# Layer 2's weights prepared during layer 1's blocks and kept in DRAM, and VectorE or GpSimd chosen operation by operation in the first block

## The chip, the core and the metric

The kernel runs on one core of a Trainium2 chip. The metric is the device time of one execution in microseconds (us). The profile is of one execution on that core. Engine names in rows: PE is TensorE, PEld its weight load, DVE is VectorE, ACT is ScalarE, POOL is GpSimd, SP is SyncE, which issues every DMA here.

## What is computed

A linear attention on 8 batches of 576 tokens (8 heads of 64), then two gated layers on the 4608 tokens, each 512 wide:

```
q_s = exp(q - max_d q);  q_s /= sum_d q_s
k_s = exp(k - max_s k);  k_s /= sum_s k_s
x   = q_s @ (k_s^T @ v)                      # per batch and head -> 4608 x 512
x   = (sigmoid(x @ w_gate) * (x @ w_val)) @ w_out      # 512 -> 1536 -> 512
h   = x @ w_in                                          # 512 -> 2048
out = ((a0 + a1 h + a2 h^2 + a3 h^3) / (1 + |b0||h| + |b1| h^2 + 1e-6)) @ w_out2
```

The layers' weights arrive as 64-bit numbers; the kernel makes 32-bit values of them with bit operations.

## The kernel before

**Products.** Each operand of a product is split into a high part (rounded by a copy on ScalarE) and a low part (value minus high part), and a product is three matmuls: high by high, low by high, high by low (`mm3`). One matmul covers 128x128 weights and 512 columns.

**Blocks and steps.** The 4608 tokens are 9 blocks of 512. In layer 1 a block has 12 steps, one for each 128 of the 1536 hidden units (`f`). Step `i` stands in this order on TensorE: the 24 matmuls of `front_a` (gate `pg` and value `pv`), what the attention of the next block puts there, and the 12 matmuls of `back_a` of the step before. Behind `front_a` come the sigmoid on ScalarE (L398), the multiplication by `pv` on VectorE (`sg`, L400, called the gate below), and the split of the result into `gh` (ScalarE) and `gl`. `pg` and `pv` have two PSUM buffers in all, so the next step's `front_a` waits for this sigmoid and this gate.

**Attention.** Blocks 1 to 7 of layer 1 also carry the attention of the block behind, in four units of two heads at fixed steps of a block (`UNIT_STEPS`). In an even step stand the exponentials of a unit (ScalarE, with a table load ahead and one behind), the normalisation of its queries on VectorE, and the maxima and subtraction of the next unit (`km`, `qm`, `q`). In the odd step behind it TensorE transposes the key maxima (`ps_kt`), multiplies keys by values (`ps_kv`), transposes the queries (`ps_qt`), runs `back_a`, and transposes the maxima back (`ps_kb`). These four share two PSUM buffers: `ps_qt` waits until VectorE has read `ps_kt` (`mx`, L281), `ps_kb` until VectorE has read `ps_kv` (`kvl`, L349).

**Weight pieces.** A piece of weights is 128 x 512. Layer 1 has 36 pieces, layer 2 has 32. Preparing one takes a load of 512 KB, an absolute value on ScalarE (L188), two TENSOR_SCALAR (L194, L197) and two SCALAR_TENSOR_TENSOR (L204, L207) on VectorE, the copy to the high part `wh` on ScalarE and the subtraction to the low part `wl` on GpSimd. Layer 1's pieces are prepared in block 0. Layer 2's are prepared in layer 1's last block (block 8), because their 64 tiles take the places of layer 1's weights in SBUF as these are used up:

```
want = 0
if j == NBLK - 2:
    want = NW1
elif j == NBLK - 1:
    want = NW1 + 3 * f + (2 if f == 0 else 1)
run(prep(min(want, NW), 3), sequence(vec, work.get(i, [])))
```

**Block 0.** Its operations (attention of blocks 0 and 1, the weights, the 12 steps) are a list with dependences; `in_time` walks through it with a cost for each kind of operation and emits the order in which every engine's queue gets its work. The engine of each kind is fixed: `wl`, `gl`, the key subtraction and the query division go to GpSimd, with the exceptions in `Q_SUB_ON_DVE` and one key subtraction.

Of the kernel before, what the change touches and what calls it, by code (L numbers as in the profile page):

```python
# [35 lines left out]
Q_SUB_ON_DVE = ((0, 0), (0, 1), (1, 0), (1, 1), (1, 2), (1, 3))  # L36
# [4 lines left out]
    "load_k": (DMA, 0.92), "load_q": (DMA, 0.74), "load_v": (DMA, 0.92), "load_w": (DMA, 1.46), "load_ab": (DMA, 0.06),  # L41
    "k_max": (DVE, 1.25), "k_t": (PE, 0.2), "k_mx": (DVE, 0.3), "k_mb": (DVE, 0.2), "k_b": (PE, 0.2),
    "k_cp": (ACT, 0.33), "k_sub": (POOL, 1.5), "k_exp": (ACT, 0.63, "exp"),
    "q_max": (DVE, 0.6), "q_sub": (POOL, 1.0), "q_exp": (ACT, 0.63, "exp"),
    "q_sum": (DVE, 0.6), "q_add": (DVE, 0.07), "q_inv": (DVE, 0.12), "q_div": (POOL, 1.0),
    "kv": (PE, 1.1), "kv_add": (DVE, 0.07), "kv_inv": (DVE, 0.12), "kv_h": (ACT, 0.4), "kv_l": (DVE, 0.4),
    "qt": (PE, 0.43), "qt_h": (ACT, 0.52), "qt_l": (DVE, 0.6),
    "x": (PE, 0.65), "x_h": (ACT, 0.52), "x_l": (DVE, 0.6),
    "xa": (PE, 0.65), "xa_out": (ACT, 0.2), "xb": (PE, 0.65), "xb_out": (ACT, 0.5),
    "w_abs": (ACT, 0.52), "w_clip": (DVE, 0.34), "w_cut": (DVE, 0.34), "w_low": (DVE, 0.6), "w_sign": (DVE, 0.6),  # L50
    "w_h": (ACT, 0.52), "w_l": (POOL, 1.23),
    "front": (PE, 1.3), "sig": (ACT, 0.48, "sigmoid"), "gate": (DVE, 0.6), "g_h": (ACT, 0.52), "g_l": (POOL, 1.23),
# [7 lines left out]
def in_time(ops, on_dve):  # L60
# [8 lines left out]
    def kind(o):  # L69
        eng, cost, table = (*KINDS[o[0]], None)[:3]  # L70
        return (DVE, DVE_COST[o[0]], table) if o in on_dve else (eng, cost, table)

    def lag(a, b):
        return 0.0 if kind(a)[0] == kind(b)[0] != DVE else LATENCY[kind(a)[0]]

    def length(o):
        if o not in rest:
            rest[o] = kind(o)[1] + max([lag(o, x) + length(x) for x in followers[o]], default=0.0)
        return rest[o]

    ready = {o: 0.0 for o, (_, after) in ops.items() if not after}
    free = dict.fromkeys(LATENCY, 0.0)
    table = "exp"
    while ready:
        starts = []
        for eng in free:
# [19 lines left out]
def kernel(ctx: ExitStack, tc: tile.TileContext, q, k, v, w1, w2, ab_in, out):  # L106
# [20 lines left out]
    ab = const.tile([P, 6], F32, name="ab")  # L127
# [14 lines left out]
    x_raw = xpool.tile([P, KC, NB], F32, name="x_raw")  # L142
    x3_d = [dram.tile([KC, P, NB], F32, name=f"x3_{j}") for j in range(NBLK)]
# [31 lines left out]
    late_pool = []  # L175
    done = [NW1] * 5
# [5 lines left out]
    def prep_abs(p):  # L182
        if p < NW1 - 2:
            val[p] = early[(p + 2) % 6]
        else:
            pool = stage if p < NW1 else late_pool[0]
            val[p] = pool.tile([P, NB], F32, tag="val", name="val", bufs=1 if p < NW1 else 4)
        nc.scalar.activation(val[p], raw[p][:, :, 1].bitcast(F32), AF.Abs)  # L188
# [22 lines left out]
    def prep_split(p):  # L211
        wt[p] = [wpool.tile([P, NB], F32R, tag="w", name=n) for n in ("wh", "wl")]
        yield from split_steps(*wt[p], val.pop(p), nc.gpsimd)

    def prep(until, times=1):

        for _ in range(times):
            jobs = []
            for n in (4, 3, 2, 1, 0):
                ready = done[n - 1] if n else len(pieces)  # L220
                if n == 0 and done[0] - done[3] >= STAGES:
                    continue
# [52 lines left out]
    def att_kt(j, u, pool, tag):  # L275
# [4 lines left out]
        mx = att.tile([P, 1], F32, tag="mx", name="mx")  # L280
# [13 lines left out]
    def att_qm(j, u):  # L294
        qm[j, u] = att.tile([P, 8], F32, tag="qm", name="qm", bufs=3)
# [100 lines left out]
    def vec_a(j, f, pg, pv):  # L396
# [8 lines left out]
        yield from split_steps(gh, gl, sg, nc.gpsimd if j in (0, NBLK - 1) and f < NF1 - 1 else nc.vector)  # L405
# [41 lines left out]
    def pool_or_dve(name):  # L447
        return nc.vector if name in on_dve else nc.gpsimd

    on_dve = {("k_sub", 0, 0)} | {("q_sub", *x) for x in Q_SUB_ON_DVE}  # L450
    banks = [("kv", 0, 0), ("qt", 0, 0)]
    for i in range(2 * NHP):
# [41 lines left out]
    for p in range(NW1):  # L494
# [5 lines left out]
        chain([("w_h", p), ("w_l", p)], prep_split(p), ("w_sign", p), p and ("w_h", p - 1))  # L500
# [27 lines left out]
    for kk in range(KC):  # L528
        chain([("next_h", kk), ("next_l", kk)], split_steps(x_h[:, kk, :], x_l[:, kk, :], x_raw[:, kk, :], nc.vector),
              ("front", NF1 - 1, KC - 1), ("xb_out", 1, kk))  # L530
# [3 lines left out]
    for o in in_time(ops, on_dve):  # L534
# [37 lines left out]

    NA = NBLK * NF1
    pend = [(0, NF1 - 1)]
    for i in range(NF1, NA):
# [14 lines left out]
        want = 0  # L590
        if j == NBLK - 2:
            want = NW1
        elif j == NBLK - 1:
            want = NW1 + 3 * f + (2 if f == 0 else 1)
        run(prep(min(want, NW), 3), sequence(vec, work.get(i, [])))
# [6 lines left out]
        if i == NA - NF1 - 2:  # L602
            att_ctx.close()
            late_pool.append(stage_ctx.enter_context(tc.tile_pool(name="late", bufs=4)))


    while done[4] < NW:
        run(prep(NW))
# [82 lines left out]
    for i in range(NBS + LAG):  # L691
        if i < NBS:
# [58 lines left out]
```

## Time and profile before

| | us |
|---|---|
| median of 3 runs | 1855.32 (1854.53 to 1855.99) |
| the profiled execution, its own time | 1856.38 |
| span of its profile | 1854.6 |
| time outside the span in that execution | 1.78 |
| TensorE busy in the span | 1783.7 |
| VectorE busy | 1224.2 |
| ScalarE busy | 1007.9 |
| GpSimd busy | 392.1 |
| granted TensorE clock, mean | 0.992 |

Engines work side by side, so busy times do not add up to the span. A matmul's duration overlaps with the next one's; the pace of TensorE is read from the starts of two matmuls and the number between them. Block 0 ends at about 185 us, block 8 of layer 1 begins at 942.17 us, and layer 2 has its first output matmul at 1077.79 us.

### The profile page before, as it was taken

The page shows a single profiled execution, that of the slowest core. Times are in us where ns is not written, and L with a number is a line of the kernel's source. Part 1 is how long each engine was busy: PE and PEld are TensorE (multiplying, and loading weights), DVE is VectorE, ACT ScalarE, POOL GpSimd, SP SyncE. Part 2 cuts the span into 40 slices and gives each one's busy share as a digit, 9 for nine tenths or more (in the row PEclk, how much of TensorE's full clock was granted, in tenths as well). Part 3 has the DMA queues.
Part 4 walks back from the last instruction along what each step waited for, and adds up shares of the span by engine and source line. Part 5 has one row for each costly group of instructions (what it writes and reads, how often), then busy time and mean ns, then how long its engine had stood idle before and what let it go on. Part 6 is the DMA issues. An engine that isn't in the chain of part 4 may idle for free.

```text
span 1854.6 us, 22112 instructions
## 1 busy us (share of the span) xinstructions
PE 1783.7 (96%) x8384; PEld 1458.1 (79%) x8384; DVE 1224.2 (66%) x1907; ACT 1007.9 (54%) x1656; POOL 392.1 (21%) x297
## 2 busy tenths in 40 slices
PE   5879999999999999999998899999999999999999
PEld 3657888888888888888876688888888888888887
DVE  9997443434344353433369988888888888787876
ACT  4546343433434343333334487777776767676765
POOL 4664000101000000100025522222222222222222
PEclk9989999999999999999999999999999999999999
DMA  5452111101011110211024210000100000000000
GB/s 203 149 166 63 63 41 44 60 23 60 21 63 41 43 60 8 77 47 46 6 96 166 102 46 24 24 24 23 46 10 37 23 23 23 23 24 23 1 23 24
DMA packets 39563, 95.97 MB, mean 52 GB/s; under 512 B 4128, under 2 KB 4128, under 8 KB 39456
## 3 DMA queue, kind: packets, MB, share of 16 engines
q1 hardware_dynamic: 39456, 94.55, 15.2%
q8 instruction: 66, 1.08, 0.2%
q14 instruction: 41, 0.34, 0.1%
HBM read 75.66 MB, written 18.87 MB: 51 GB/s over the span
## 4 chain that ended last, share of the span: by engine, by line
PE 83%; DVE 12%; issue 3%; ACT 2%; DMA 1%; POOL 0%; DVEq 0%; ACTq 0%; SPq 0%
PE accb L672 21%; PE acc L414 13%; PE ph L155 7%; PE ph L157 7%; PE ph L156 7%; PE pv L155 4%; PE pv L157 4%; PE pg L155 4%; PE pv L156 4%; PE pg L156 4%; PE pg L157 4%; DVE sg L400 1%; DVE early L207 1%; DVE val L194 1%; DVE early L204 1%
## 5 line engine op out<-in xcount | busy, mean ns | idle before, releaser
L148 POOL TENSOR_TENSOR glb<-gb,ghb 128x512 fp32r<-128x512 f32 x144 | 186.8, 1297 | 594.3 <-ACT ghb L146 594.3
L400 DVE TENSOR_TENSOR sg<-pv,sg 128x512 f32<-128x512 f32 x108 | 74.4, 689 | 332.2 <-PE pv L157 171.3
L398 ACT ACTIVATE sg<-pg 128x512 f32<-128x512 f32 x108 | 64.4, 596 | 363.1 <-PE pg L157 359.4
L640 ACT ACTIVATE h<-ph 128x512 f32<-128x512 f32 x144 | 86.1, 598 | 197.1 <-PE ph L157 195.9
L155 PE MATMUL pv<-x_h,wh 128*128 128x512 f32 x432 | 172.3, 399 | 17.6 <-DVE sg L400 17.5
L155 PE MATMUL pg<-x_h,wh 128*128 128x512 f32 x432 | 175.1, 405 | 13.5 <-ACT sg L398 13.3
L308 POOL TENSOR_TENSOR k<-k,kma 128x640 f32<-128x640 f32 x29 | 46.4, 1600 | 599.2 <-ACT kma L291 599.2
L157 PE MATMUL pg<-x_l,wh 128*128 128x512 f32 x432 | 170.6, 395 | 0.9 <-DVE x_l L381 0.9
L157 PE MATMUL pv<-x_l,wh 128*128 128x512 f32 x432 | 171.0, 396 | 0.0
L156 PE MATMUL pv<-x_h,wl 128*128 128x512 f32 x432 | 170.9, 396 | 0.0
L156 PE MATMUL pg<-x_h,wl 128*128 128x512 f32 x432 | 170.8, 395 | 0.0
L672 PE MATMUL accb<-wl,ghb 128*128 128x512 f32 x576 | 158.3, 389 | 0.0
L672 PE MATMUL accb<-wh,ghb 128*128 128x512 f32 x576 | 158.3, 389 | 0.0
L672 PE MATMUL accb<-wh,glb 128*128 128x512 f32 x576 | 158.3, 389 | 0.0
L643 DVE SCALAR_TENSOR_TENSOR ah<-h,babs,ah 128x512 f32<-128x512 f32 x144 | 107.9, 749 | 53.8 <-ACT ah L641 53.8
L414 PE MATMUL acc<-gh,wh 128*128 128x512 f32 x432 | 125.5, 400 | 3.6 <-DVE x_raw L420 2.0
L155 PE MATMUL ph<-x_h,wh 128*128 128x512 f32 x320 | 124.6, 389 | 2.0 <-ACT x_h L146 2.0
L672 PEld LDWEIGHTS accb<-wh,glb 128*128 128x128 f32 x576 | 108.2, 188 | 22.4
L672 PEld LDWEIGHTS accb<-wl,ghb 128*128 128x128 f32 x576 | 108.1, 188 | 22.5
L672 PEld LDWEIGHTS accb<-wh,ghb 128*128 128x128 f32 x576 | 108.1, 188 | 22.4
L659 DVE SCALAR_TENSOR_TENSOR u<-ah,r 128x512 f32<-128x512 f32 x144 | 99.4, 690 | 39.5 <-ACT r L649 39.5
L157 PE MATMUL ph<-x_l,wh 128*128 128x512 f32 x320 | 124.6, 390 | 0.0
(118 smaller groups left out, 4045.3 us busy)
## 6 DMA issues: line engine op xcount, KB each, us to landing
raw<-in_w SPq DMA_DIRECT2D x68, 512.0 KB, 3.7
v<-in_v SPq DMA_DIRECT2D x30, 325.0 KB, 3.0
k<-in_k SPq DMA_DIRECT2D x30, 320.0 KB, 3.5
q<-in_q SPq DMA_DIRECT2D x36, 256.0 KB, 3.6
x<-x_raw SPq DMA_DIRECT2D x36, 256.0 KB, 2.2
x_raw<-x SPq DMA_DIRECT2D x9, 1024.0 KB, 5.5
out<-ob SPq DMA_DIRECT2D x36, 256.0 KB, 2.4
x_raw<-in_v SPq DMA_DIRECT2D x2, 325.0 KB, 4.9
```

What stands on the lines that cost most here:

```text
L148: lo_eng.tensor_tensor(out=lo, in0=src, in1=f32(h), op=ALU.subtract)
L155: nc.tensor.matmul(ps, wh, xh, start=first, stop=False)
L156: nc.tensor.matmul(ps, wl, xh, start=False, stop=False)
L157: nc.tensor.matmul(ps, wh, xl, start=False, stop=last)
L308: eng.tensor_tensor(out=t, in0=t, in1=kmt[j, u].unsqueeze(1).to_broadcast([P, KCH, P]), op=ALU.subtract)
L398: nc.scalar.activation(sg, pg, AF.Sigmoid)
L400: nc.vector.tensor_tensor(out=sg, in0=pv, in1=sg, op=ALU.mult)
L414: nc.tensor.matmul(accs["a", j][m], x[:, m * P:(m + 1) * P], y, start=(f == 0 and n == 0), stop=(f == NF1 - 1 and n == 2))
L640: nc.scalar.activation(h2, ph, AF.Square)
L643: nc.vector.scalar_tensor_tensor(out=ah, in0=h2, scalar=babs[:, 1:2], in1=ah, op0=ALU.mult, op1=ALU.add)
L659: nc.vector.scalar_tensor_tensor(out=u, in0=ah, scalar=q_one, in1=r, op0=ALU.add, op1=ALU.mult)
L672: nc.tensor.matmul(accs["b", j][t], x[:, t * P:(t + 1) * P], y, start=(f == 0 and n == 0), stop=(f == NF2 - 1 and n == 2))
```

## The change

**Layer 2's weights.** The 32 pieces are prepared during blocks 1 to 7, from step 14 of layer 1 on, one piece every two and a half steps: the load in its first step, the absolute value and the two TENSOR_SCALAR in the second, the two SCALAR_TENSOR_TENSOR, the high copy and the low subtraction (GpSimd) in the third. High and low part go into one staging tile `hl`, which a DMA writes to DRAM (`w2_d`). In block 8, when the tiles of layer 1's weights come free, `fetch` reads them back with two DMAs a piece; the last three pieces are fetched at layer 2's first step. The pool `late` and the preparation in block 8 go away.

**Block 0.** The costs in `KINDS` are other numbers, and six kinds (`k_sub`, `q_sub`, `q_div`, `w_l`, `g_l`, `next_l`) have a cost for VectorE and one for GpSimd. `in_time` takes the engine on which an operation would end first and notes it in `chosen`; `Chosen` emits it there. Four tiles are made larger (`ab`, `v`, `mx`, and one more buffer for `qm`).

```
-Q_SUB_ON_DVE = ((0, 0), (0, 1), (1, 0), (1, 1), (1, 2), (1, 3))
...
+    "w_h": (ACT, 0.62), "w_l": ({DVE: 0.7, POOL: 1.29},),
+    "g_l": ({DVE: 0.7, POOL: 1.29},),
...
+        for t, eng, mine in sorted(starts, key=lambda x: x[0]):
+            mine = [
+                o for o in mine
+                if all(t + engines(o)[eng] <= max(free[e], at(o, e)) + c for e, c in engines(o).items())]
+            if mine:
+                break
...
+    w2_d = [dram.tile([P, 2, NB], F32, name=f"w2_{p}") for p in range(2 * NF2)]
...
+    def prep_split(p, eng=nc.gpsimd):
+        if p < NW1:
+            wt[p] = [wpool.tile([P, NB], F32R, tag="w", name=n) for n in ("wh", "wl")]
+            yield from split_steps(*wt[p], val.pop(p), eng)
+        else:
+            hl = stage.tile([P, 2, NB], F32R, tag="raw", name="hl")
+            yield from split_steps(hl[:, 0], hl[:, 1], val.pop(p), nc.gpsimd)
+            yield
+            nc.sync.dma_start(out=w2_d[p - NW1], in_=f32(hl))
+
+    def fetch(p):
+        wt[p] = [wpool.tile([P, NB], F32R, tag="w", name=n) for n in ("wh", "wl")]
+        for n in range(2):
+            nc.sync.dma_start(out=f32(wt[p][n]), in_=w2_d[p - NW1][:, n])
+
+    def prep(stage_of):
+        for p, n in stage_of:
+            yield from (prep_load, prep_abs, prep_bits_a, prep_bits_b, prep_split)[n](p) or ()
+            yield
...
+    prep_at = {}
+    for p in range(NW1, NW):
+        at0 = NF1 + 2 + 5 * (p - NW1) // 2
+        for n, step in enumerate((0, 1, 1, 2, 2)):
+            prep_at.setdefault(at0 + step, []).append((p, n))
...
-        run(prep(min(want, NW), 3), sequence(vec, work.get(i, [])))
+        run(prep(prep_at.get(i, [])), sequence(vec, work.get(i, [])))
...
+        if j == NBLK - 1:
+            while len(wt) < NW and order1[len(wt) - NW1][0] < f - 1:
+                fetch(len(wt))
```

**Where it moves instructions.** In block 0 GpSimd has 64 operations before: 36 `wl`, 11 `gl`, 8 query divisions, 2 query subtractions and 7 key subtractions. With the change it has 46: 23, 10, 2, 5 and 6. The other 18 stand on VectorE.

The first place is ScalarE's queue in step 28 (block 2, an even step). Before (L398 is first the sigmoid, then the table load for the next one; `x_raw` is the attention's output, `k` and `q` the exponentials):

```order
L398 ACTIVATE sg<-pg 128x512
L146 ACTIVATE gh<-sg 128x512
L383 ACTIVATE x_raw<-ps_xt 128x192
L383 ACTIVATE x_raw<-ps_xt 128x320
L312 ACT_TABLE_LOAD
L312 ACTIVATE k<-k 128x640
L304 ACTIVATE q<-q 128x512
L398 ACT_TABLE_LOAD
```

With the change (ScalarE, the same step):

```order
L413 ACTIVATE sg<-pg 128x512
L160 ACTIVATE gh<-sg 128x512
L398 ACTIVATE x_raw<-ps_xt 128x192
L160 ACTIVATE hl<-val 128x512
L398 ACTIVATE x_raw<-ps_xt 128x320
L327 ACT_TABLE_LOAD
L327 ACTIVATE k<-k 128x640
L319 ACTIVATE q<-q 128x512
L413 ACT_TABLE_LOAD
```

The high copy of a weight piece (`hl`) now stands ahead of the table load and the exponentials, and it needs both SCALAR_TENSOR_TENSOR of its piece.

The second place is VectorE's queue in step 31 (block 2, an odd step). Before:

```order
L400 TENSOR_TENSOR sg<-pv,sg 128x512
L281 TENSOR_REDUCE mx<-ps_kt 128x1
L283 COPY km<-mx 128x128
L148 TENSOR_TENSOR gl<-sg,gh 128x512
L338 TENSOR_SCALAR rs<-ps_kv 128x1
L340 RECIPROCAL rs<-rs 128x1
L349 SCALAR_TENSOR_TENSOR kvl_105<-ps_kv,rs,kvh_97 64x64 x2
L364 TENSOR_TENSOR ql<-ps_qt,qh 128x512
```

With the change (VectorE, the same step):

```order
L415 TENSOR_TENSOR sg<-pv,sg 128x512
L296 TENSOR_REDUCE mx<-ps_kt 128x1
L298 COPY km<-mx 128x128
L215 SCALAR_TENSOR_TENSOR val<-raw,val 128x512
L218 SCALAR_TENSOR_TENSOR val<-raw,val 128x512
L162 TENSOR_TENSOR gl<-sg,gh 128x512
L353 TENSOR_SCALAR rs<-ps_kv 128x1
L355 RECIPROCAL rs<-rs 128x1
L364 SCALAR_TENSOR_TENSOR kvl_105<-ps_kv,rs,kvh_97 64x64 x2
L379 TENSOR_TENSOR ql<-ps_qt,qh 128x512
```

Two operations on a weight piece now stand ahead of `gl`, `rs` and `kvl`.

The third place is VectorE's queue at the end of block 0. Before, ahead of the block's last gate (the last row):

```order
L319 TENSOR_SCALAR qs<-qs 128x8
L321 RECIPROCAL qs<-qs 128x8
L338 TENSOR_SCALAR rs<-ps_kv 128x1
L400 TENSOR_TENSOR sg<-pv,sg 128x512
L340 RECIPROCAL rs<-rs 128x1
L349 SCALAR_TENSOR_TENSOR kvl_105<-ps_kv,rs,kvh_97 64x64 x2
L364 TENSOR_TENSOR ql<-ps_qt,qh 128x512
L338 TENSOR_SCALAR rs<-ps_kv 128x1
L340 RECIPROCAL rs<-rs 128x1
L364 TENSOR_TENSOR ql<-ps_qt,qh 128x512
L349 SCALAR_TENSOR_TENSOR kvl_106<-ps_kv,rs,kvh_98 64x64 x2
L400 TENSOR_TENSOR sg<-pv,sg 128x512
```

With the change (VectorE, the rows ahead of the same gate):

```order
L472 TENSOR_TENSOR wl<-val,wh 128x512
L205 TENSOR_SCALAR val<-val 128x512
L208 TENSOR_SCALAR val<-val 128x512
L353 TENSOR_SCALAR rs<-ps_kv 128x1
L215 SCALAR_TENSOR_TENSOR val<-raw,val 128x512
L355 RECIPROCAL rs<-rs 128x1
L218 SCALAR_TENSOR_TENSOR val<-raw,val 128x512
L379 TENSOR_TENSOR ql<-ps_qt,qh 128x512
L364 SCALAR_TENSOR_TENSOR kvl_106<-ps_kv,rs,kvh_98 64x64 x2
L472 TENSOR_TENSOR x_l<-x_raw,x_h 128x512 x3
L415 TENSOR_TENSOR sg<-pv,sg 128x512
```

Before, the last weight operation stands 13 rows ahead of the last gate (just ahead of these rows), with another gate between; now it stands four rows ahead of the last gate, with no gate between.

## Rows read from the trace of the kernel before

**Rows 1.** The page, part 1 (busy us, share, instructions) and VectorE's line of part 2.
```profile
PE 1783.7 (96%) x8384; PEld 1458.1 (79%) x8384; DVE 1224.2 (66%) x1907; ACT 1007.9 (54%) x1656; POOL 392.1 (21%) x297
DVE  9997443434344353433369988888888888787876
```

**Rows 2.** Stretches; columns: length, each engine's busy us, PEclk, DMA share, GB/s.
```profile
185.00:942.17 757.17, 751.17 (x3821) 619.64 (x3820) 303.58 (x577) 283.65 (x475) 37.70 (x24) 1.00 0.13 43
920.00:940.00 20.00, 20.00 (x92) 16.52 (x91) 3.65 (x6) 4.46 (x9) 0.00 (x0) 1.00 0.00 0
1000.00:1020.00 20.00, 16.66 (x70) 12.49 (x68) 19.86 (x24) 8.63 (x15) 11.31 (x8) 1.00 0.55 192
```

**Rows 3.** Timeline of TensorE, layer 1's last block and the first output step of layer 2.
```profile
934.01 0.39 PE L155 MATMUL pg<-x_h,wh 128*128 128x512 f32 x1
...
942.17 0.39 PE L155 MATMUL pg<-x_h,wh 128*128 128x512 f32 x1
...
1077.79 1.07 PE L672 MATMUL accb<-wh,ghb 128*128 128x512 f32 x4
```

**Rows 4.** What TensorE waited for, 940 to 1080 us; us in total, times, longest.
```profile
PE pv L155 <- DVE sg L400: 7.7, 6, 1.9
```

**Rows 5.** VectorE by line and shape, 0 to 166 us; busy us, mean ns, idle before.
```profile
L207 DVE SCALAR_TENSOR_TENSOR early<-raw,early 128x512 uint32<-128x512 uint32 x34 | 34.3, 1015 | 0.0
L204 DVE SCALAR_TENSOR_TENSOR early<-raw,early 128x512 uint32<-128x512 uint32 x34 | 27.2, 804 | 0.0
L194 DVE TENSOR_SCALAR early<-early 128x512 f32<-128x512 f32 x34 | 24.2, 718 | 0.0
L197 DVE TENSOR_SCALAR early<-early 128x512 uint32<-128x512 uint32 x34 | 23.8, 704 | 0.1
```

**Rows 6.** L194 on VectorE over the whole span; duration ns as minimum, median, maximum.
```profile
L194 DVE TENSOR_SCALAR early<-early x34: 366/416/1670, 22.8 to 145.3; 128x512 f32<-128x512 f32 x34
L194 DVE TENSOR_SCALAR val<-val x34: 414/1502/1535, 152.0 to 1057.6; 128x512 f32<-128x512 f32 x34
```

**Rows 7.** Timeline of VectorE at the end of block 0.
```profile
166.55 0.68 DVE L207 SCALAR_TENSOR_TENSOR val<-raw,val 128x512 uint32<-128x512 uint32 x1
...
183.12 0.69 DVE L400 TENSOR_TENSOR sg<-pv,sg 128x512 f32<-128x512 f32 x1 [1.24 <-ACT sg L398]
183.78 1.29 DVE L148 TENSOR_TENSOR x_l<-x_raw,x_h 128x512 fp32r<-128x512 f32 x2
```

**Rows 8.** The stretch between those operations, columns as in Rows 2.
```profile
167.23:183.12 15.89, 15.89 (x110) 12.95 (x109) 4.55 (x16) 10.74 (x20) 5.09 (x4) 1.00 0.20 60
```

**Rows 9.** What TensorE waited for, 0 to 170 us.
```profile
PE pg L155 <- ACT sg L398: 10.1, 5, 3.2
PE pv L155 <- DVE sg L400: 9.8, 5, 2.8
```

**Rows 10.** Timeline of ScalarE in a step with exponentials, block 1.
```profile
226.95 0.64 ACT L383 ACTIVATE x_raw<-ps_xt 128x128 f32<-128x128 f32 x2
227.61 1.28 ACT L312 ACT_TABLE_LOAD   x1
```

**Rows 11.** Timeline of VectorE in that step and the one behind it.
```profile
225.69 0.69 DVE L400 TENSOR_TENSOR sg<-pv,sg 128x512 f32<-128x512 f32 x1 [5.71 <-ACT sg L398]
...
230.20 0.69 DVE L317 TENSOR_REDUCE qs<-q 128x8 f32<-128x512 f32 x1 [2.42 <-ACT q L304]
...
234.78 0.69 DVE L400 TENSOR_TENSOR sg<-pv,sg 128x512 f32<-128x512 f32 x1 [0.18 <-PE ps_kt L278]
...
236.16 0.69 DVE L148 TENSOR_TENSOR gl<-sg,gh 128x512 fp32r<-128x512 f32 x1 [0.24 <-ACT gh L146]
...
237.88 0.58 DVE L349 SCALAR_TENSOR_TENSOR kvl<-ps_kv,rs,kvh 64x64 fp32r<-64x64 f32 x2 [0.76 <-ACT kvh L345]
```

**Rows 12.** Timeline of TensorE in the step behind it.
```profile
235.81 0.63 PE L357 MATMUL ps_qt<-ident,q 128*128 128x128 f32 x4 [0.30 <-DVE mx L281]
...
239.05 0.27 PE L288 MATMUL ps_kb<-ident,km 128*128 128x128 f32 x1
```

More of the change, by code (lines that the diff above doesn't have):

```diff
@@ L67, in in_time, with engines, table_of, at @@
     rest, end = {}, {}
[L69 to L74, printed above, removed]
+    def engines(o):
+        kind = KINDS[o[0]]
+        return kind[0] if isinstance(kind[0], dict) else {kind[0]: kind[1]}
+    def table_of(o):
+        return (*KINDS[o[0]], None, None)[2] if isinstance(KINDS[o[0]][0], str) else None
     def length(o):
         if o not in rest:
-            rest[o] = kind(o)[1] + max([lag(o, x) + length(x) for x in followers[o]], default=0.0)
+            rest[o] = min(engines(o).values()) + max([0.2 + length(x) for x in followers[o]], default=0.0)
         return rest[o]
-    ready = {o: 0.0 for o, (_, after) in ops.items() if not after}
+    ready = {o: (0.0, None) for o, (_, after) in ops.items() if not after}
     free = dict.fromkeys(LATENCY, 0.0)
     table = "exp"
+    def at(o, eng):
+        t, by = ready[o]
+        return t if by != eng or eng == DVE else t - LATENCY[eng]
     while ready:
@@ L126 @@
     make_identity(nc, ident)
-    ab = const.tile([P, 6], F32, name="ab")
+    ab = const.tile([P, 70], F32, name="ab")[:, :6]
     babs = const.tile([P, 2], F32, name="babs")
@@ L185, in prep_abs @@
         else:
-            pool = stage if p < NW1 else late_pool[0]
-            val[p] = pool.tile([P, NB], F32, tag="val", name="val", bufs=1 if p < NW1 else 4)
+            val[p] = stage.tile([P, NB], F32, tag="val", name="val", bufs=1)
         nc.scalar.activation(val[p], raw[p][:, :, 1].bitcast(F32), AF.Abs)
@@ L404, in vec_a @@
         g_t["a", j, f] = (gh, gl)
-        yield from split_steps(gh, gl, sg, nc.gpsimd if j in (0, NBLK - 1) and f < NF1 - 1 else nc.vector)
+        late = nc.gpsimd if j == NBLK - 1 and f < NF1 - 1 else nc.vector
+        yield from split_steps(gh, gl, sg, late if j else Chosen(("g_l", f)))
     def back_a(j, f):
@@ L445, in also, with __init__, tensor_tensor @@
         ops[name][1].extend(a for a in after if a)
-    def pool_or_dve(name):
-        return nc.vector if name in on_dve else nc.gpsimd
-    on_dve = {("k_sub", 0, 0)} | {("q_sub", *x) for x in Q_SUB_ON_DVE}
+    chosen = {}
+    class Chosen:
+        def __init__(self, name):
+            self.name = name
+        def tensor_tensor(self, **kw):
+            (nc.vector if chosen[self.name] == DVE else nc.gpsimd).tensor_tensor(**kw)
     banks = [("kv", 0, 0), ("qt", 0, 0)]
@@ L533 @@
     op(("load_q", 2, 0), partial(load_q, 2, 0), ("qt", 1, 2))
[L534 removed]
+    for o in in_time(ops, chosen):
         ops[o][0]()
@@ L691 @@
     for i in range(NBS + LAG):
+        while len(wt) < NW and i >= 0 and order1[len(wt) - NW1][0] < NF1 + i - 1:
+            fetch(len(wt))
         if i < NBS:
```

85 lines of the change are left out of this document (31 added, 54 removed).

## The prediction

> **What bounds the kernel now.** I first read the page's first part for the engine that could pace the whole span, and there TensorE is busy for 96% while VectorE has 66% [rows 1]. That share is an average over stages, so the slices of VectorE come next: its line reads 9997 at the start and a run of nines and eights about the middle, and threes and fours between [rows 1]. There are thus three kinds of stretch. From 185 to 942 us, blocks 1 to 7, TensorE is busy for 751.17 of 757.17 us [rows 2]: it is the bound, and what VectorE saves there is worth nothing. The last 20 us ahead of block 8's weights show the same in small, with VectorE busy 3.65 of 20 us and TensorE all of it [rows 2]. From 1000 to 1020 us, in the stretch where layer 2's weights are prepared, it is the other way: VectorE has 19.86 of 20 us, TensorE 16.66 [rows 2], and TensorE's waits name the gate on VectorE, 7.7 us [rows 4]. In the first block TensorE waits 10.1 us for sigmoids and 9.8 us for gates [rows 9]. So two stretches of the three can give time, and blocks 1 to 7 can only lose it.
>
> **Term 1: the switch of layers.** The timeline of TensorE gives its pace: a step of 36 matmuls runs from 934.01 to 942.17 us [rows 3], 8.16 us or 0.2267 us each. From there to layer 2's first output matmul, at 1077.79 us, are 135.62 us [rows 3], and in them, counted from the loops, 492 matmuls: 12 times 24 of `front_a`, 13 backs of 12, and four fronts of layer 2 with 12 each. At that pace they take 111.5 us. The excess, 24.1 us, is all that the stretch can give. The change takes from VectorE four operations for each of 32 pieces there, and puts two DMAs a piece in their place. Are these hidden? From 942 us they have 11 steps of 8.16 us for 29 pieces of 512 KB: 15.2 MB in 90 us, 169 GB/s, and the chip moved 192 GB/s from 1000 to 1020 us with the DMA engines busy for 0.55 [rows 2]. The fetches are issued from SP, whose queue then holds nothing else but waits for steps of TensorE that lie behind. They need no engine for bits, so no gate can be late for them. I take all 24.1 us; the bounds are 22 (a first fetch that is late, about a quarter of a step) and 24.1.
>
> **Term 2: block 0.** Each line on weights has 34 instructions of the same size in the table by shape, at 1015, 804, 718 and 704 ns, together 109.5 us [rows 5]. Undisturbed they cost less: the TENSOR_SCALAR's median is 416 ns [rows 6], and a SCALAR_TENSOR_TENSOR at the end of the block takes 0.68 us [rows 7], which makes 34 x (2 x 0.416 + 2 x 0.68) = 74.5 us. The excess is 35.0 us. What it is shows in L194, where in block 8, beside GpSimd's work on every piece, the median is 1502 ns against 414 at the least [rows 6]: an operation that meets GpSimd is held for 1.09 us. With 64 operations on GpSimd in block 0 the excess is 35.0/64 = 0.55 us for each, a lower bound, since other lines of VectorE can be held too; the upper bound is one hold of 1.09 us for each. I take 0.70, near the lower one, which is measured in this block. The change moves 18 operations: -18 x 0.70 = -12.6 us. They go to VectorE, where a second subtraction behind a first adds 1.29 - 0.69 = 0.60 us [rows 7]: +10.8. Net -1.8 us, between +0.9 and -8.8.
>
> The Trainium skill (Perfetto Trace Analysis, section Optimizing Scalar/DVE Operations) says that with a saturated VectorE it may make sense to offload work, even to GpSimd, but that the two share a port so that it might not help. By its first half moving work onto VectorE costs time (rival (c), 1846), by the row it does not (1834). The trace's 1502 against 414 ns agrees with the second half.
>
> Then the order. Before, the last operation on a weight ends at 167.23 us and the block's last gate comes at 183.12 [rows 7]. In these 15.89 us VectorE is busy for 4.55 [rows 8]: 11.3 us idle, while TensorE, never idle there [rows 8], works off matmuls that earlier waits put off. With the change the last weight operation stands four rows ahead of the last gate, so the weights reach into this hole, and TensorE must do earlier what it does there now. At most 11.3 us come out, if all the work ahead is paced by VectorE; nothing, if the weights are only later and the gates with them. TensorE's 19.9 us of waits for sigmoids and gates [rows 9] leave room for it. I take half, -5.6. **Block 0 sums to -7.4**, from +0.9 to -20.1.
>
> **Term 3: blocks 1 to 7.** 32 pieces now stand there with four operations on VectorE, two on ScalarE and one on GpSimd each. In 757 us VectorE is busy for 303.58 and ScalarE for 283.65 [rows 2], so most pieces hide beside TensorE. The DMAs do too: load and store of 32 pieces are 33.5 MB in some 650 us, 52 GB/s on top of 43 [rows 2]. What counts is where an attention unit has no slack. The step with exponentials has next to none: VectorE waits 2.42 us for `q`, then works without a gap up to the next gate, which has waited 0.18 us for TensorE, and TensorE waits 0.30 us for `mx` behind it [rows 11, 12]. So whatever delays the exponentials by more than 0.18 us is paid in full.
>
> In six steps (16, 18, 28, 66, 76, 78) the high copy `hl` stands ahead of the table load. It needs both SCALAR_TENSOR_TENSOR behind the gate: 225.69 + 0.69 + 2 x 0.68 = 227.7 us [rows 7, 11]. A ScalarE operation on 128x512 takes about 0.64, as the two parts of `x_raw` do together, and the larger of these parts (0.2 to 0.4) follows; the table load stands at 227.61 [rows 10] and would come at 228.5, 0.9 later. Less 0.18 that is 0.7 each, 4.2 us. In two more (26, 38) no attention output stands there, and `wl` on GpSimd can meet the normalisation: one hold of 1.09 us each [rows 6], 2.2 at most, which I take. In six odd steps (31, 41, 43, 51, 53, 63) the two SCALAR_TENSOR_TENSOR precede `gl`, `rs` and `kvl`: 1.36 us, of which the 0.24 that `gl` waits for `gh` [rows 11] swallow a part, so `kvl` ends 1.12 later. It ends at 237.88 + 0.58 = 238.46 for a `ps_kb` at 239.05 [rows 11, 12]: 0.59 of slack, and 0.53 are left, 3.2 us in all. The other pieces stand in steps with room: an absolute value or a TENSOR_SCALAR fits into the 2.42 us ahead of `qs`. **Together +9.6 us.** Nothing is the lower bound, if the tile framework's releases leave more slack than one step's timeline shows; 18.3 is the upper, if a hold of 1.09 [rows 6] comes on top in each of the eight steps with exponentials.
>
> Larger tiles alone: no row shows a duration that would depend on them; 0.
>
> **Sum.** 1856.38 (the profiled execution's own time) - 24.1 - 7.4 + 9.6 = 1834.5. The profiled run is 1.06 above the median of 1855.32, so in terms of the median 1833.4; I say 1834.
>
> **Rivals.** (a) The pieces hide wholly in blocks 1 to 7. For it speaks the half-empty VectorE there, against it the 0.18 us of slack [rows 11]. 1834 - 9.6 = 1824. (b) Block 0 gains at its upper end, with 1.09 for each GpSimd operation taken away and the whole hole filled; for it speak the 2.8 to 3.2 us of the longest waits [rows 9], against it the 0.55 that the block's own rows give. 1834 - 12.7 = 1821. (c) In block 0 the holds stay, because the 46 operations left meet a VectorE that is even fuller, and the 18 moved cost their full 0.60: 1834 + 12.6 = 1846 or 1847. The slices of 9 at the start [rows 1] speak for it. (d) The change doesn't do at the switch what it says: fetches come late since tiles come free late, and half of the 24.1 stays: 1846. Against it are DMA queues that moved nothing from 920 to 940 us [rows 2]. (e) **The other side:** every `wl` on GpSimd in blocks 1 to 7 holds a VectorE operation on the path. 32 x 1.09 = 34.9 in place of 9.6 gives 1859. It decides from (24.1 + 7.4) / 32 = 0.98 us of delay a piece. Against it: TensorE's pace leaves VectorE idle for 60% of the time there [rows 2], so most holds fall where nobody waits.
>
> **How the numbers follow.** The sum has 54%, with a range of its own of 1827 to 1842 (term 3 between 3 and 18, the others as taken). (a) has 15%, (b) 12, (c) 12, (d) 3, (e) 4. The range from 1820 to 1848 leaves out (e), and the edges of (a), (b) and (c) where they fall together. A measurement of this kernel tells apart about 0.2%, 3.7 us; only (e) and half of a mixture of (c) and (d) come near or over 1851. So faster 0.94, same 0.02, slower 0.04.
>
> **What would show it.** Term 1 is right if in block 8 no wait of TensorE for `pv` is left and the first output matmul comes 111 to 114 us after the block's first `pg`. Term 2 is right if the first gate of block 1 comes 4 to 10 us earlier, with the weight lines of VectorE in block 0 at a lower mean than 1015 to 704 ns, and little idle time of VectorE ahead of the last gate. Term 3 is right if TensorE's waits in blocks 1 to 7 grow from 6 to some 15 us, on `ps_qt` and `ps_kb`. The forecast is wrong if block 0 does not shorten (c), if the waits in blocks 1 to 7 pass 31 us (e), or if SP's fetches hold TensorE in block 8 (d).

## The result and the profile after

The changed kernel takes 1835.44 us in the median of 4 runs (1834.72 to 1837.36), before 1855.35: a ratio of 0.9895, 95% interval 0.9877 to 0.9912. The forecast was 1834, in a range from 1820 to 1848. The profiled execution takes 1834.72 us with a span of 1832.9, 21.7 less than before.

The first part of its page and VectorE's line of the second, which answer to [rows 1]:

```profile
PE 1772.1 (97%) x8384; PEld 1452.7 (79%) x8384; DVE 1182.3 (65%) x1925; ACT 1005.6 (55%) x1652; POOL 363.3 (20%) x279
DVE  9998545445455454454430288888888888887876
```

The slices between the nines at the start and layer 2 now read fours and fives where they read threes and fours, and the digits 699 of block 8 have become 302: layer 2's weights have left block 8 and lie in blocks 1 to 7.

Three stretches (columns as in [rows 2]): up to the end of the last operation on a layer 1 weight, from there to block 0's last gate, and from block 8's first matmul to layer 2's first output matmul:

```profile
0.00:170.20 170.20, 130.29 (x647) 99.45 (x648) 161.29 (x280) 92.45 (x160) 80.92 (x67) 0.91 0.48 159
170.20:174.38 4.18, 3.81 (x19) 2.93 (x17) 2.98 (x7) 4.13 (x8) 1.78 (x1) 1.00 0.00 0
945.02:1056.54 111.52, 111.52 (x494) 92.34 (x492) 22.87 (x36) 28.70 (x47) 15.43 (x12) 1.00 0.54 181
```

The two ends of the last one in the timeline of TensorE, as in [rows 3]:

```profile
945.02 0.39 PE L169 MATMUL pg<-x_h,wh 128*128 128x512 f32 x1
...
1056.54 1.07 PE L698 MATMUL accb<-wh,ghb 128*128 128x512 f32 x4
```

Before, the same way took 135.62 us [rows 3]; it takes 111.52 now, TensorE is busy for every bit of it, and VectorE for 22.87. That is 24.10 us less. Block 8 starts 2.85 us later than before (945.02 against 942.17). The first gate of block 1 comes at 180.30 us, 10.39 earlier than the 190.69 of before and just past the 4 to 10 that the prediction named as its sign. So blocks 1 to 7 lose 10.39 + 2.85 = 13.24 us. The three together make 21.25; the last 0.45 of the 21.7 come in layer 2.

What TensorE waited for from 200 to 940 us (us in total, times, longest):

```profile
PE ps_qt L372 <- DVE mx L296: 12.3, 18, 1.1
PE ps_kb L303 <- DVE kvl L364: 3.7, 7, 1.2
```

Before, the one wait in blocks 1 to 7 was `ps_qt` on `mx`, 6.0 us. In place of it there are now 16.0, and two smaller rows of 0.5 together.

VectorE by line and shape up to 170.2 us, as in [rows 5]:

```profile
L215 DVE SCALAR_TENSOR_TENSOR early<-raw,early 128x512 uint32<-128x512 uint32 x34 | 31.8, 935 | 0.0
L218 DVE SCALAR_TENSOR_TENSOR early<-raw,early 128x512 uint32<-128x512 uint32 x34 | 30.5, 898 | 0.0
L205 DVE TENSOR_SCALAR early<-early 128x512 f32<-128x512 f32 x34 | 20.6, 613 | 0.3 <-ACT early L199 0.2
L208 DVE TENSOR_SCALAR early<-early 128x512 uint32<-128x512 uint32 x34 | 19.8, 582 | 0.0
```

The four lines take 102.7 us where they took 109.5 [rows 5]. Three have a lower mean; that of the first SCALAR_TENSOR_TENSOR rose, from 804 to 935 ns. With the last two pieces it is 107.4 us against 118.6.

**Where the 13.24 us stand.** The gates give a measure for each step: the time of a gate less that of the same gate before, and how this difference changes from one step to the next. The loss of a step shows in the gate of the step behind it.

| steps | what was forecast there | forecast, us | measured, us |
|---|---|---|---|
| 16, 18, 28, 66, 76, 78 | high copy ahead of the exponentials | 4.2 | 0.89 + 0.90 + 0.87 + 0.67 + 0.54 + 0.56 = 4.43 |
| 26, 38 | GpSimd holds the normalisation | 2.2 | 1.04 + 1.03 = 2.07 |
| 31, 41, 43, 51, 53, 63 | two operations ahead of `kvl` | 3.2 | 0.61 + 0.60 + 0.61 + 0.65 + 0.61 + 0.65 = 3.73 |
| 27, 62, 72 | nothing | 0 | 1.40 + 1.15 + 0.95 = 3.50 |
| all others together | nothing | 0 | -0.49 |

The first kind, in the timeline of ScalarE of the changed kernel, step 16 (start, length, and in brackets the idle time before and what ended it):

```profile
216.50 0.26 ACT L398 ACTIVATE x_raw<-ps_xt 128x128 f32<-128x128 f32 x1
217.29 0.63 ACT L160 ACTIVATE hl<-val 128x512 fp32r<-128x512 f32 x1 [0.53 <-DVE val L218]
217.83 0.47 ACT L398 ACTIVATE x_raw<-ps_xt 128x384 f32<-128x384 f32 x1
218.32 1.28 ACT L327 ACT_TABLE_LOAD   x1
```

`hl` waits 0.53 us for VectorE's second SCALAR_TENSOR_TENSOR, the rest of `x_raw` waits behind it, and the table load starts at 218.32. The step's gate starts at 215.24, 3.08 us ahead of that; before, it was 1.92 (225.69 to 227.61) [rows 10, 11].

The second kind, in step 26, is one operation on VectorE and one on GpSimd, from their two timelines:

```profile
312.53 1.21 DVE L334 TENSOR_SCALAR qs<-qs 128x8 f32<-128x8 f32 x1
```

```profile
312.43 1.29 POOL L162 TENSOR_TENSOR hl<-val,hl 128x512 fp32r<-128x512 f32 x1 [8.19 <-issue]
```

The same operation in step 16, with GpSimd idle:

```profile
221.62 0.17 DVE L334 TENSOR_SCALAR qs<-qs 128x8 f32<-128x8 f32 x1
```

The TENSOR_SCALAR on 128x8 takes 0.17 us where nothing holds it. In step 26 it takes 1.21 and ends when GpSimd's subtraction does, at 313.7: 1.04 us, which is the whole loss of the step. The Trainium skill (SBUF — State Buffer, section Who interferes with whom) says that a TENSOR_SCALAR can take the port pair that VectorE shares with GpSimd, and that who comes second is blocked for the whole instruction; the trace agrees, with these two ends at the same time.

The last kind was not foreseen. In the timeline of SP's queue (step 26) and of ScalarE (step 27):

```profile
298.88 0.43 SPq L275 DMA_DIRECT2D q<-in_q  x1
...
313.74 0.33 SPq L230 DMA_DIRECT2D w<-hl  x1
314.12 0.42 SPq L192 DMA_DIRECT2D raw<-in_w  x1
```

```profile
318.76 0.67 ACT L199 ACTIVATE val<-raw 128x512 f32<-128x512 f32 x1 [2.91 <-DMA raw<-in_w]
319.33 0.62 ACT L160 ACTIVATE gh<-sg 128x512 fp32r<-128x512 f32 x1
```

SP issues nothing from 299.3 to 313.74. Its next command is the store of piece `hl`, which waits for the low subtraction on GpSimd that ends at 313.72; the load of the next piece's `raw` stands behind the store. Issued at 314.12, it lands 4.6 us later. ScalarE waits 2.91 us for it, with `gh` queued behind the absolute value.

### The profile page after: what moved, and what is told of

It is laid out like the page before. It is cut to its first block, busy times and chain, and to the rows that moved or that the text cites. A ratio compares the mean times of both kernels' runs of the same rounds, so it can differ in the third digit from the quotient of the medians.

```text
span 1832.9 us, 22295 instructions
## 1 busy us (share of the span) xinstructions
PE 1772.1 (97%) x8384; PEld 1452.7 (79%) x8384; DVE 1182.3 (65%) x1925; ACT 1005.6 (55%) x1652; POOL 363.3 (20%) x279
## 4 chain that ended last, share of the span: by engine, by line
PE 56%; DVE 0%; ACT 0%; issue 0%
PE accb L698 21%; PE ph L171 7%; PE ph L170 7%; PE ph L169 7%; PE acc L430 4%; PE pg L169 1%; PE pv L169 1%; PE pg L171 1%; PE pv L171 1%; PE pg L170 1%; PE pv L170 1%; PE ps_qt L372 0%; PE ps_xt L170 0%; PE ps_xt L169 0%; PE ps_xt L171 0%; DVE km L287 0%
## 5 line engine op out<-in xcount | busy, mean ns | idle before, releaser
L162 POOL TENSOR_TENSOR hl<-val,hl 128x512 fp32r<-128x512 f32 x32 | 41.3, 1290 | 475.1 <-ACT hl L160 224.3
L430 PE MATMUL acc<-gh,wl 128*128 128x512 f32 x432 | 122.4, 395 | 5.0 <-POOL wl L472 5.0
```

Of the source, the lines that this page charges most:

```text
L162: lo_eng.tensor_tensor(out=lo, in0=src, in1=f32(h), op=ALU.subtract)
L430: nc.tensor.matmul(accs["a", j][m], x[:, m * P:(m + 1) * P], y, start=(f == 0 and n == 0), stop=(f == NF1 - 1 and n == 2))
```

## Experiments

**The two parts apart.** One kernel has the new preparation and block 0 exactly as before (every engine's order in block 0 is that of before), the other the new block 0 with layer 2's weights in block 8 as before:

```diff
 # e1_switch_alone: after.py with before's KINDS, in_time and
-            (nc.vector if chosen[self.name] == DVE else nc.gpsimd).tensor_tensor(**kw)
+            (nc.vector if self.name in on_dve | always else nc.gpsimd).tensor_tensor(**kw)
 # e2_block0_alone: before.py with after's KINDS, in_time, Chosen
```

> The new preparation of layer 2's weights with block 0 as before. If the three stretches add up independently, the first gate of block 1 comes at 190.7 us as before, blocks 1 to 7 lose the 13.2 us that they lose in the changed kernel, and block 8 gains 24.1: 1855.3 - 24.1 + 13.2 = 1844 to 1845 us. Rival: the loss in blocks 1 to 7 belongs to what block 0's new schedule leaves behind (work pushed past its end), then this kernel comes to 1831 to 1836.

> The new block 0 scheduler alone, layer 2's weights prepared in block 8 as before. If the stretches are independent: first gate of block 1 at 180.3 us (10.4 earlier than before), blocks 1 to 7 without new waits (6.0 us as before), 1845 us. Rival: the time won in block 0 is lost again later (the 6 us of waits in blocks 1 to 7 grow, or block 8 waits longer): 1850 to 1855.

Measured: 1846.19 us for the first (ratio 0.9948, 0.9934 to 0.9963) and 1843.64 for the second (0.9936, 0.9919 to 0.9952). In the first the gate of block 1 stands 0.65 us later than before, blocks 1 to 7 lose 14.1 us in the same steps with about the same amounts (only step 72 loses clearly more, 1.58), and the last stretch wins what it won. In the second the gate comes 10.7 us earlier, and at the end of block 7 that distance is the same to 0.02 us. The first is 1.2 us above the range expected, the second 1.4 below the figure expected; both are far from their rivals, which fall: the stretches add up. The sum of the two gains, 9.7 + 12.2, is 21.9 against 19.9 of both together, a difference within the intervals.

**The pieces in quiet steps.** Same operations and engines, but each layer 2 piece is prepared whole within one step that has no exponentials and no key-value products, with its load issued two steps ahead:

```diff
-        at0 = NF1 + 2 + 5 * (p - NW1) // 2
-        for n, step in enumerate((0, 1, 1, 2, 2)):
-            prep_at.setdefault(at0 + step, []).append((p, n))
+    quiet = [i for i in range(NF1 + 9, NF1 * (NBLK - 1)) if i % NF1 in (0, 1, 9, 10, 11)]
+    for p, step in zip(range(NW1, NW), quiet):
+        prep_at.setdefault(step - 2, []).insert(0, (p, 0))
+        prep_at.setdefault(step, []).extend((p, n) for n in (1, 2, 3, 4))
```

> The changed kernel with each layer 2 piece prepared within one step that holds no exponentials and no key-value products (the steps 9, 10, 11 of a block and 0, 1 of the next), its load two steps ahead; same number of operations, same engines. If the 13.2 us of blocks 1 to 7 come from where the operations stand in the queues of ScalarE and VectorE, they go nearly all: 1822 to 1825 us, waits of TensorE in blocks 1 to 7 back at 6 to 8 us. Rival: they come from the amount of work, GpSimd's holds and DMA traffic anywhere: 1830 to 1836.

Measured: 1822.65 us (0.9819, 0.9804 to 0.9833). Blocks 1 to 7 take 0.27 us less than before the change, and TensorE's waits from 200 to 940 us are one row:

```profile
PE ps_qt L372 <- DVE mx L296: 6.0, 18, 0.4
```

It is the row of the kernel before, to the number. So the work itself costs nothing there; its place in the queues did.

**Loads a step earlier.**

```diff
-        for n, step in enumerate((0, 1, 1, 2, 2)):
+        for n, step in enumerate((-1, 1, 1, 2, 2)):
```

> The changed kernel with each layer 2 piece's load issued one step earlier. In three steps (27, 62, 72) an absolute value on ScalarE waits 1.5 to 3.7 us for its load, which was issued behind the store of the piece before, and the split of gate results or the exponentials queue behind it; these steps cost 1.40 + 1.15 + 0.95 us. If the order in SP's queue does it, these three go: 1831 to 1832 us. Rival: the load is slow because DMA queues are shared, then the same steps still wait: 1834 to 1836.

Measured: 1830.93 us (0.9867, 0.9852 to 0.9882). Blocks 1 to 7 lose 9.81 us in place of 13.24. The three losses are gone and the other fourteen stay within 0.06 us. SP's queue in the stretch shown above is now this:

```profile
298.88 0.43 SPq L192 DMA_DIRECT2D raw<-in_w  x1
...
313.19 0.33 SPq L230 DMA_DIRECT2D w<-hl  x1
```

The load goes out 15 us earlier, ahead of the store that waits. The rival, DMA queues that are shared, falls.

**The split alone a step later** (on top of the earlier loads):

```diff
-        for n, step in enumerate((-1, 1, 1, 2, 2)):
+        for n, step in enumerate((-1, 1, 1, 2, 3)):
```

> The early-load kernel (1830.93 us) with only the split of each layer 2 piece moved one step later, so that the high copy never stands between a gate and the exponentials behind it; the two SCALAR_TENSOR_TENSOR stay where they are. If the copy, which waits for these two, is what delays the exponentials in steps 16, 18, 28, 66, 76 and 78, their six losses (0.5 to 0.9 each, 4.4 in all) go, those in the steps 31, 41, 43, 51, 53 and 63 (0.6 each) stay: 1826 to 1828 us. Rival: the two VectorE operations delay the exponentials' step by themselves, then 1830 to 1832.

Measured: 1826.49 us (0.9841, 0.9825 to 0.9857); blocks 1 to 7 lose 5.43. The six losses of the high copy are gone, and those of step 26 and 38 as well, since their split has moved too; the six at `kvl` stay (0.57 to 0.64). New ones stand in steps 42, 52 and 62 (0.99, 0.82, 0.46). ScalarE and VectorE in step 42:

```profile
452.61 0.63 ACT L160 ACTIVATE hl<-val 128x512 fp32r<-128x512 f32 x1
453.40 0.63 ACT L160 ACTIVATE gh<-sg 128x512 fp32r<-128x512 f32 x1 [0.16 <-DVE sg L415]
...
454.70 0.69 ACT L199 ACTIVATE val<-raw 128x512 f32<-128x512 f32 x1 [0.39 <-POOL hl L162]
```

```profile
454.06 1.15 DVE L162 TENSOR_TENSOR gl<-sg,gh 128x512 fp32r<-128x512 f32 x1 [0.70 <-ACT gh L160]
```

And GpSimd:

```profile
453.37 1.29 POOL L162 TENSOR_TENSOR hl<-val,hl 128x512 fp32r<-128x512 f32 x1 [4.33 <-DVE sg L415]
```

`val` has one buffer: the next piece's absolute value now waits for the low subtraction on GpSimd (0.39 us), and `gl`, 0.69 us long elsewhere, is held to 1.15. The copy that waits was the cause of the six losses; moving it made smaller waits of another kind, 2.3 us for the 6.4 saved. That the time lies in the range expected is in part luck: the 2.0 us saved in steps 26 and 38 and the 2.3 lost in the new places, neither of them forecast, cancel.

**Layer 2's low subtraction on VectorE**, in the changed kernel:

```diff
-            yield from split_steps(hl[:, 0], hl[:, 1], val.pop(p), nc.gpsimd)
+            yield from split_steps(hl[:, 0], hl[:, 1], val.pop(p), nc.vector)
```

> The changed kernel with the low subtraction of layer 2's pieces on VectorE in place of GpSimd. In steps 26 and 38 a TENSOR_SCALAR on 128x8 is held by GpSimd for 1.04 us on the path; there the subtraction itself (0.60) takes its place: 0.9 us less in all. Elsewhere GpSimd holds nothing that is waited for, so nothing is won: 1833.5 to 1835.5. Rival: GpSimd's holds lie behind more of the 13.2 us, then 1828 to 1832.

Measured: 1832.69 us (0.9876, 0.9859 to 0.9892), 0.7 to 0.8 us from either range. Blocks 1 to 7 lose 11.69, 1.55 less. The two steps with a hold fall from 1.04 and 1.03 to 0.46 each, which is 1.15 of it; step 62 falls from 1.15 to 0.58. The theory's two steps were right, but not that nothing else would move: GpSimd lies behind some 2.6 of the 13 us (2.07 in the two holds, 0.57 in step 62), and not behind most of them.

**What decides block 0.** Four kernels on top of the quiet steps, each with another part of the scheduler changed:

```diff
 # e5_wl_pool
-    "w_h": (ACT, 0.62), "w_l": ({DVE: 0.7, POOL: 1.29},),
+    "w_h": (ACT, 0.62), "w_l": (POOL, 1.29),
 # e6_wl_vector
+    "w_h": (ACT, 0.62), "w_l": (DVE, 0.7),
 # e7_fixed_engines: the new numbers, each kind on its engine of before
+        if o in FIXED_DVE:
+            return {DVE: 0.83 if o[0] == "k_sub" else 0.7}
 # e8_old_costs: the numbers of before, and where a kind may choose
+    "w_h": (ACT, 0.52), "w_l": ({DVE: 0.6, POOL: 1.23},),
```

> The quiet-steps kernel (1822.65 us, first gate of block 1 at 182.0 us) with all 36 low subtractions of layer 1's weights on GpSimd: some 54 operations there in block 0 in place of 46. Theory: an operation moved between the two engines costs VectorE about as much as its hold, so block 0 moves by at most 2 us: 1821 to 1825. Rival: each operation on GpSimd holds VectorE for 1.0 to 1.1 us against 0.6 for its own, then 8 more cost 3.5 to 4 us: 1826 to 1827.

> The quiet-steps kernel with all 36 low subtractions of layer 1's weights on VectorE: some 26 operations on GpSimd in block 0 in place of 46. Theory (moving one costs VectorE 0.1 to 0.2 us net, as 18 moved ones made it busy 3 us longer up to the last weight operation): 1824 to 1827 us, first gate of block 1 at 184 to 187. Rival one, holds at 1.0 to 1.1 us each: 20 fewer give 8 to 10 us, 1813 to 1815. Rival two, holds that stay whatever is moved: 20 x 0.6 = 12 us more, 1834.

> The quiet-steps kernel with every kind of operation of block 0 on the engine that it had before (64 on GpSimd), but with the new cost numbers, which set the order. Theory: block 0's gain is the order, weight operations reaching into VectorE's idle stretch ahead of the last gate, and the choice of engine is worth little: first gate of block 1 at 180 to 184 us, 1821 to 1825. Rival: the gain is the relief from holds, then block 0 is as before: gate at 190, 1830 to 1831.

> The quiet-steps kernel with the new choice of engine in block 0, but the cost numbers of before (VectorE's costs 0.6 and 0.73 for the kinds that may choose). Theory (the order, set by the numbers, is the gain): the first gate of block 1 at 187 to 190 us, 1828 to 1831. Rival (the choice is the gain): 180 to 183 us, 1821 to 1824.

Then two more, with the numbers of before and `w_l` on VectorE, and with all six kinds on VectorE:

```diff
 # e9_old_costs_wl_vector
-    "w_h": (ACT, 0.52), "w_l": ({DVE: 0.6, POOL: 1.23},),
+    "w_h": (ACT, 0.52), "w_l": (DVE, 0.6),
 # e10_all_vector
-    "q_max": (DVE, 0.68), "q_sub": ({DVE: 0.7, POOL: 1.05},), "q_exp": (ACT, 0.63, "exp"),
+    "q_max": (DVE, 0.68), "q_sub": (DVE, 0.7), "q_exp": (ACT, 0.63, "exp"),
```

> The quiet-steps kernel with the new choice, the old cost numbers, and all low subtractions of layer 1's weights on VectorE: some 22 operations on GpSimd in block 0. The four weight lines' time on VectorE fell by 0.72 us for each operation taken from GpSimd in the kernels with 64, 54, 46, 34 and 26 of them; with 22 it should be 88 us. Each moved one costs 0.60 to 0.70 itself, so little changes against the two kernels at 1819.7: 1817 to 1820. Rival: old numbers and this move add their gains in full, 3 us each: 1816 or less.

> The quiet-steps kernel with nothing of block 0 on GpSimd. If holds are the whole excess of the weight lines, their time falls to 36 x 2.05 to 2.15 = 74 to 77 us, no TENSOR_SCALAR takes longer than 0.5 us, and the other work moved (0.60 to 0.83 each) takes back what is won: 1817 to 1823 us. Rival: VectorE's durations stay long for another reason than GpSimd, then 1830 or more.

| kernel | on GpSimd in block 0 | weight lines on VectorE, us | last weight operation ends | first gate of block 1 | median, us (ratio, interval) |
|---|---|---|---|---|---|
| before | 64 | 118.6 | 167.23 | 190.69 | 1855.35 |
| new numbers, engines fixed (e7) | 64 | 118.8 | 175.65 | 188.29 | 1828.72 (0.9854, 0.9840 to 0.9869) |
| `w_l` on GpSimd (e5) | 54 | 111.7 | 172.25 | 182.56 | 1823.44 (0.9825, 0.9809 to 0.9841) |
| quiet steps (e3) | 46 | 106.5 | 171.93 | 181.99 | 1822.65 (0.9819, 0.9804 to 0.9833) |
| old numbers, with choice (e8) | 34 | 95.1 | 166.83 | 178.58 | 1819.65 (0.9804, 0.9789 to 0.9819) |
| `w_l` on VectorE (e6) | 26 | 91.1 | 165.22 | 176.17 | 1819.69 (0.9803, 0.9789 to 0.9818) |
| old numbers, `w_l` on VectorE (e9) | 23 | 85.4 | 166.03 | 177.41 | 1817.44 (0.9794, 0.9779 to 0.9808) |
| all on VectorE (e10) | 0 | 78.9 | 166.28 | 175.63 | 1817.62 (0.9797, 0.9782 to 0.9811) |

The weight lines' time is the sum of the four lines over all 36 pieces. All rows but the first have the quiet steps, so they differ from one another in block 0 alone. The new block 0 of the changed kernel was profiled in six kernels (the changed one, e2, e3, e4, e11, e12), with the gate at 180.30, 179.99, 181.99, 179.76, 179.73 and 179.47 us, so what is under 2.5 us in that column says nothing. The mean granted clock up to the last weight operation was 0.91, 0.90, 0.95, 0.90, 0.98 and 0.98 in them, and the gate does not follow it.

Against what was expected: e5, e9 and e10 lie in their ranges. e6, at 1819.69 us with the gate at 176.17, lies outside its own (1824 to 1827) and outside both rivals': moving work to VectorE paid, by less than rival one. e7, at 1828.72, lies nearer to its rival (1830 to 1831) than to its theory, and e8, at 1819.65, is faster than even its rival's 1821. In e10 the weight lines take 78.9 us where 74 to 77 were expected; that is 36 pieces at 2.19 us, the undisturbed price that the prediction used.

The theory that I went in with, that block 0's gain is the order and not the choice of engine, fell in both kernels made to test it. With the new numbers alone, VectorE's idle stretch at the end does shrink, as these two stretches of e7 show (up to the last weight operation, and from there to the last gate):

```profile
0.00:175.65 175.65, 129.06 (x615) 98.32 (x616) 162.94 (x259) 93.31 (x158) 98.48 (x85) 0.94 0.48 154
175.65:182.37 6.72, 6.70 (x51) 5.39 (x49) 3.39 (x9) 5.75 (x11) 1.28 (x1) 1.00 0.00 0
```

Before, the second was 15.89 us long with 4.55 busy [rows 8]; it is 6.72 with 3.39. But the last weight operation comes 8.4 us later, and block 1's first gate only 2.4 earlier. The choice on top of it (e3) brings 6.3 us, or up to 8.8 by the other kernels with this block 0; the choice with the numbers of before (e8) brings 12.1 in all. No kernel has fixed engines and the numbers of before under the new `in_time`, so what the new walk by itself brings is not shown apart. The same two stretches of e3:

```profile
0.00:171.93 171.93, 132.54 (x647) 101.88 (x648) 160.54 (x280) 92.36 (x160) 81.10 (x67) 0.95 0.48 157
171.93:176.10 4.17, 3.77 (x19) 2.91 (x17) 2.97 (x6) 4.12 (x8) 1.79 (x1) 1.00 0.00 0
```

VectorE is busy for 162.94 of 175.65 us in e7 and for 160.54 of 171.93 in e3. To compare the same work, these are the stretches up to block 1's first gate, before, in e7, in e3 and in the changed kernel:

```profile
0.00:190.69 190.69, 145.71 (x690) 110.29 (x691) 167.00 (x271) 103.87 (x176) 103.66 (x86) 0.94 0.44 142
0.00:188.29 188.29, 141.68 (x690) 108.48 (x691) 168.40 (x270) 101.52 (x174) 99.76 (x86) 0.95 0.45 143
0.00:181.99 181.99, 142.18 (x690) 109.56 (x691) 165.60 (x289) 98.95 (x172) 82.89 (x68) 0.95 0.45 148
0.00:180.30 180.30, 140.00 (x690) 107.15 (x691) 166.35 (x289) 99.05 (x172) 82.71 (x68) 0.91 0.46 150
```

VectorE's busy time is 167.00, 168.40, 165.60 and 166.35 us, its idle time 23.7, 19.9, 16.4 and 14.0. So of the 6.3 us that the choice brings, 2.8 are less to do on VectorE, and 3.5 are idle time. The weight lines (third column of the table) show why it has no more to do although 18 operations were added to it. The line of the first TENSOR_SCALAR in the changed kernel, and in the kernel with nothing on GpSimd (minimum, median, maximum in ns):

```profile
L205 DVE TENSOR_SCALAR early<-early x34: 400/416/1529, 24.1 to 150.9; 128x512 f32<-128x512 f32 x34
```

```profile
L205 DVE TENSOR_SCALAR early<-early x34: 416/423/433, 27.3 to 145.1; 128x512 f32<-128x512 f32 x34
```

With GpSimd at work the median is undisturbed and the maximum 1529; without it none of the 34 takes over 433.

## Why the prediction was right, and where it was not

**The switch of layers** was right to 0.1 us: 24.1 forecast, 24.10 measured, and with no wait left in block 8. The count of matmuls by the pace of an undisturbed step gave the floor, and the stretch went down to it. Rival (d) falls: 111.52 us with TensorE busy throughout.

**Block 0** won 10.4 us in place of 7.4, within the bounds, but by other parts than forecast. I sized the exchange of engines at -1.8 and the filled hole at -5.6. The price of a GpSimd operation was about right: 0.70 taken, and in the weight lines before against after gives 11.2 / 18 = 0.62, e7 against e3 12.3 / 18 = 0.68, e3 against e6 15.4 / 20 = 0.77. So was the net of the exchange: VectorE's busy time up to block 1's first gate fell by 0.7 us in the changed kernel and by 1.4 in e3. The step that failed is the one behind it. The idle time was credited to the order; e7 shows that the order alone fills the hole with work that is later by 8.4 us and brings 2.4 at block 1's gate, near the lower bound that the prediction named ("nothing, if the weights are only later and the gates with them"). The choice of engine was worth 6.3 us where I gave it 1.8: the last weight operation comes 3.7 us earlier, and 2.6 more come between it and the gate. Why VectorE's idle time falls with the choice stays open; that work no longer waits for a slower GpSimd is a guess that no run separates. The granted clock has no visible part in it, as the six kernels with the same block 0 show.

Rival (b) had the sign of the correction, with too high a price. Rival (c), moved operations at their full price on a full VectorE, falls: every kernel with fewer operations on GpSimd was as fast or faster, down to none at all. The first half of what the prediction cites from the Trainium skill (Perfetto Trace Analysis, section Optimizing Scalar/DVE Operations), that offloading from a full VectorE may make sense, is not borne out here: the last kernel, with nothing offloaded, is among the two fastest, at 1817.62 us.

**Blocks 1 to 7** lost 13.24 us in place of 9.6. The fourteen steps named ahead lost 10.2 (4.43 + 2.07 + 3.73), in the places forecast. For the first eight the mechanism is shown too. e12 takes away the six of the high copy by moving the split, and e11, with the low subtraction on VectorE, leaves these six as they are, so it is the copy. e11 takes away the two holds, but for the 0.46 us that VectorE now spends itself. The six at `kvl` rest on TensorE's waits for it and on e3, which takes all away at once. The timeline of one step with its slack of 0.18 and 0.59 us was enough for these sizes. The missing 3.5 us come from the sentence "The DMAs do too". It weighed bytes per microsecond, and those were no limit. It did not ask what a load stands behind in SP's queue. A store that waits for GpSimd stands there, and the load behind it came so late for its absolute value that three steps paid; ScalarE waited for a late load in steps 37 and 87 too (2.4 and 2.6 us), where it cost nothing. Rival (a), all hidden, is what e3 makes true by moving the pieces; rival (e), 1.09 us for every piece, falls: GpSimd's hold is on the path in two steps of the 32 pieces.

The errors of the terms, 3.0 too little gain and 3.6 too little loss, nearly cancel; the profiled execution, 1834.72 us, is 0.2 from the forecast sum of 1834.5, and the median 1.4 from the forecast. That is closer than the terms deserve.

**A version that beats both** is e9, 1817.44 us, or e10, 1817.62: pieces in quiet steps and little or nothing on GpSimd in block 0. They are not told apart.

## What to carry to other kernels

Price a moved step at the places where its neighbours have no slack, one queue at a time, and take in the queue that issues DMAs: a store that waits for a result holds every load behind it, however idle the DMA engines are. When VectorE is full and GpSimd beside it, count what each GpSimd operation costs VectorE before counting what it saves; here the two were about equal, and the simplest placement, everything on VectorE, was as good as any choice tried. An idle stretch at the end of a stage is not a gain in hand, since filling it with work can make that work late.

## What the runs showed of the hardware

A TENSOR_SCALAR of 0.17 us took 1.21 beside one GpSimd subtraction of 1.29. VectorE's four weight lines, 78.9 us with GpSimd silent, were longer in every kernel with GpSimd at work: by 6.5 us with 23 operations on it, 12.2 with 26, 16.2 with 34, 27.6 with 46, 32.8 with 54 and 39.9 with 64. That is 0.28, 0.47, 0.48, 0.60, 0.61 and 0.62 us for each. That the price of one is higher where there are more I had not expected. But the 23 and the 26 hold no `wl`, and the order of the work differs too, so the runs don't tell whether it is the number, the kind or the place that sets the price.

The hold goes the other way as well. This is GpSimd in e9, then VectorE in the same stretch:

```profile
63.66 7.80 POOL L471 TENSOR_TENSOR gl<-sg,gh 128x512 fp32r<-128x512 f32 x1 [27.51 <-PE acc L429]
```

```profile
69.62 0.69 DVE L471 TENSOR_TENSOR wl<-early,wh 128x512 fp32r<-128x512 f32 x1
72.12 0.69 DVE L414 TENSOR_TENSOR sg<-pv,sg 128x512 f32<-128x512 f32 x1 [1.81 <-ACT sg L412]
```

Up to 70.31 us VectorE ran its weight operations one behind the other at their undisturbed lengths (0.42 and 0.69 us). The subtraction on GpSimd, 1.29 us long elsewhere, took 7.80 and ended 1.15 us after the last of them. By these records GpSimd waited here and VectorE did not, so the price of a GpSimd operation is not one number.
